# A fused attention and two-layer expert kernel: the issue order read from a table

## The chip, the cores and the metric

The kernel runs on one core of a Trainium2 chip. It is one program for five engines: TensorE (matmuls), VectorE (DVE in the rows), ScalarE (ACT), GpSimd (POOL) and SyncE (SP, which issues most DMAs); GpSimd issues a few DMAs too. Each engine takes its instructions in the order in which they are written, and waits where one needs what another engine has not finished. The metric is the device time of one execution in microseconds.

## The reference

```python
# attention, q, k, v: (4 batches, 8 heads, 576, 64)
q_d = q.reshape(B, H, 144, 4, D).mean(axis=3)          # k_d, v_d alike
out_up = np.repeat(sm_attn(q_d, k_d, v_d), 4, axis=2)   # softmax attention on 144 positions
mask = np.abs(pos[:, None] - pos[None, :]) < 4          # local attention
out_local = softmax(where(mask, q @ k.T / 8, -1e9)) @ v
x = (out_up + out_local)                                # -> (2304, 512)
h = (x @ w1) * (x @ w2) @ w3                            # w1, w2: 512x1024, w3: 1024x1024
y = h @ w_out                                           # w_out: 1024x512
z = maximum(maximum(y @ m1, y @ m2), y @ m3)            # 512x768 each
result = z @ m_out                                      # 768x512
```

The weights come as 64-bit numbers; the kernel turns them into 32-bit ones itself.

## The kernel before

All numbers are 32 bits wide. A matmul of full accuracy is written as three, of a high and a low part of each operand (`mm3`, L421 to L424), so most work goes in threes, 504 columns of x at a time (4 chunks of 504 and one of 288).

The program is built twice over. First Python code walks through the work and adds some 2,500 *tasks* to a list (`Program.add`), each with an engine, a cost, a function that issues its instructions, and the tasks it depends on. Then `Program.order` decides in which order the tasks are issued, and the functions are called in that order. So the place of an instruction in the code says nothing about when it runs. `order` in this kernel is a list scheduler: it steps through planned time, and each engine takes the ready task with the earliest due time; the due times come from a backward pass and a table of shifts, one for each group of tasks (`SHIFTS`).

The stages of work:

- *Tiles of the down-sampled attention* (`down`, one for each batch and pair of heads, sixteen in all). One `qk` load (576 KB); a `vd` tile that is loaded once by SP and then added to three times by accumulating DMAs of GpSimd (L476); the copies `q` and `k` (ScalarE, L484), the sums `qk` (VectorE, L489 and L491), scores `sp` on TensorE (L501), maxima (L511), `two`, which holds four maxima and sums for each row (L514, L525, L527), the exponentials (L518), scaling `e` (L531), transposes `pp` (L540), output `po` (L550).
- *Slabs of the local attention* (`slab`, three a batch, 192 columns each): value loads (`v` and `vl`), scores `sq` (L604), softmax on VectorE and ScalarE, transposes `ptq` (L630), outputs `poq` (L649), sum with the tile's output (L658), and the split into high and low part, `xt` (L415 on ScalarE, L417 on VectorE).
- *W' = w3 @ w_out* (`weights_product`), which replaces two matmuls of the reference by one: twelve weight blocks of 128x1024 (`raw`, loaded 512 KB at a time) are converted (`float32`, L442 on ScalarE, L443 to L448 on VectorE) into `wf`, and sixteen products `pw` (L711) of four logical matmuls (eight instructions) each are summed in two halves; each half is then split into `wp`.
- *First layer*: for each chunk and each of eight blocks f, `pf` (two matmul groups, `front`), their product `g`, and `py` (`back`), with weights `w` that `pair` converts. The first `pf` needs x of columns 0 to 503, that is the first three slabs, and the first pair of weights.
- *Second layer*: weights `cv` are converted, summed and written to memory (`convert`), fetched again (`wu`), and used in products `pb` (`halves_front`, `rest_front`), and at the end `final` with `gg` and `wm`.

Tasks marked `chained` (the products of W', of the first layer and of the second) depend on the one added before: they run on TensorE in the order in which they are added, W' first. All matmuls of the attention are free to stand between them.

Buffers: four PSUM banks for sums and four for the rest in the first stages; two `qk` buffers, three `vd` buffers, six places for raw weight blocks, two places for a slab's values. A load into a buffer waits on its queue until the buffer's last reader is done, and whatever stands behind it on that queue waits too.

Of the kernel before, what the change touches and what calls it, by code (L numbers as in the profile page):

```python
# [17 lines left out]
HP = H // 2  # L18
# [49 lines left out]
ROUNDS_PLAIN = 6  # L68

SHIFTS = {  # L70
# [72 lines left out]
class Task:  # L143
    __slots__ = ("n", "options", "fn", "deps", "nexts", "late", "end", "size", "takes", "tiles", "group", "count")


class Program:


    AFTER = {"PE": 0.30, "DVE": 0.12, "ACT": 0.15, "POOL": 0.15, "SP": 2.2}  # L150
    RATE = 0.32e6
    ADDS = 2.3

    HAND, COME = 165, 70

    def __init__(self):
        self.tasks, self.chain, self.group = [], None, 0

    def add(self, options, fn, reads=(), writes=(), chained=False, size=0, count=0):
# [3 lines left out]
        t.n, t.options, t.fn, t.size, t.group = len(self.tasks), options, fn, size, self.group  # L163
        t.count = count
        t.nexts, t.end, t.late, t.takes, t.tiles = [], None, None, [], []
        deps = set()
# [28 lines left out]
    def order(self, rounds=ROUNDS_PLAIN):  # L195

        ts = self.tasks
        for t in ts:
            for d in t.deps:
                ts[d].nexts.append(t.n)  # L200
        for t in reversed(ts):
            t.late = min((ts[n].late - self.lag(t, t.options, n) for n in t.nexts), default=0.0)
            t.late -= min(c for _, c in t.options) + t.size / self.RATE
        best = None
        for n in range(rounds):
            done, places = self.forward()
            end = max(t.end for _, _, t, _ in done)
            if best is None or end < best[0]:
                best = end, done, places, [t.late for t in ts]
            self.backward(done)  # L210
        for t, late in zip(ts, best[3]):
            t.late = late + SHIFTS.get(t.group, 0.0)
        best = None, *self.forward()
        for x, slot in best[2]:
            x.slot = slot
        return [(t, e) for _, _, t, e in sorted(best[1], key=lambda d: d[:2])]

    def lag(self, task, options, n):

        (e, _), *more = options  # L220
        if task.size:
            return self.AFTER["SP"] + (self.ADDS if e == "POOL" else 0.0)
        to = self.tasks[n].options
        return 0.0 if not more and len(to) == 1 and e == to[0][0] != "SP" else self.AFTER[e]

    def backward(self, done):
        ts = self.tasks
        on = {t.n: e for _, _, t, e in done}
        left = [len(t.nexts) for t in ts]
        by = [0.0] * len(ts)  # L230
        free, queue = dict.fromkeys(self.AFTER, 0.0), 0.0
        can = {e: [n for n in on if on[n] == e and not left[n]] for e in self.AFTER}
        for _ in ts:
            now, e, n = None, None, None
            for o, ns in can.items():
                if ns:
                    at = min(free[o], max(by[n] for n in ns))
                    if now is None or at > now:
                        now, e = at, o
            n = max((n for n in can[e] if by[n] >= now), key=lambda n: (ts[n].end, n))  # L240
            t = ts[n]
            can[e].remove(n)
            cost = dict(t.options)[e]
            if t.size:
                queue = min(queue, now) - t.size / self.RATE
                t.late = queue - cost
                free[e] = min(free[e], now) - cost
            else:
                t.late = free[e] = now - cost
            for d in t.deps:  # L250
                left[d] -= 1
                by[d] = min(by[d], t.late - self.lag(ts[d], [(on[d], 0)], n))
                if not left[d]:
                    can[on[d]].append(d)

    def forward(self):
        ts = self.tasks
        for t in ts:
# [4 lines left out]
        left = [len(t.deps) for t in ts]  # L263
        can = {e: set() for e in self.AFTER}
        free = dict.fromkeys(can, 0.0)
        ready = [0.0] * len(ts)
        queue = 0.0
        hand, since = self.HAND, 0.0
        places, done = [], []

        def offer(t):
            for e, _ in t.options:
                can[e].add(t.n)

        def start(n):
            t = ts[n]
            if t.count:
                return max(free["PE"], begin(n), since + (t.count - hand) / self.COME - t.options[0][1])
            return begin(n)

        def begin(n):
            t = ts[n]
            if not t.takes:
                return ready[n]
            return max(ready[n], sorted(s.free for s in t.takes[0].among)[len(t.takes) - 1])

        for t in ts:
            if not t.deps:
                offer(t)
        while len(done) < len(ts):  # L290
            best = None
            for e, ns in can.items():
                if not ns:
                    continue
                at = {n: start(n) for n in ns}
                now = max(free[e], min(at.values()))
                if now < 1e9 and (best is None or now < best[0]):
                    best = now, e, min((n for n in ns if at[n] <= now), key=lambda n: (ts[n].late, n))
            now, e, n = best
            t = ts[n]  # L300
            if len(t.options) > 1:

# [9 lines left out]
            for o, _ in t.options:  # L312
                can[o].discard(n)
# [15 lines left out]
            for m in t.nexts:  # L329
                left[m] -= 1  # L330
                ready[m] = max(ready[m], end + self.lag(t, [(e, 0)], m))
                if not left[m]:
                    offer(ts[m])
# [867 lines left out]
```

## Time and profile before

| what | value |
|---|---|
| runs | 780.63, 780.65, 784.3 us; median 780.65 |
| profiled execution, span | 781.2 us |
| TensorE (PE) busy | 734.0 us, 94% |
| VectorE busy | 482.0 us, 62% |
| ScalarE busy | 324.1 us, 41% |
| GpSimd busy | 53.7 us, 7% |
| chain that ended last | PE 83%, DVE 6%, DMA 5%, ACT 2%, issue 1%, SPq 1% |
| DMA | 126.99 MB, mean 163 GB/s |

The profiled execution's own time is its span, from the first instruction to the last. Busy time is the share in which an engine worked; a wait in the timeline stands in brackets behind the instruction that ended it, with what it waited for. One logical matmul of W' shows as two instructions. An average over the span hides that the engines are loaded differently early and late, so the rows below are by stretch.

### The profile page before, as it was taken

How to read it: one execution, taken by the hardware profiler on the slowest of the kernel's cores; microseconds unless marked ns; L12 is line 12 of the kernel's file. 1: busy time of each engine (PE TensorE's matmuls, PEld its weight loads, DVE VectorE, ACT ScalarE, POOL GpSimd, SP SyncE). 2: the span in 40 equal slices, each digit the busy share in tenths (PEclk: the TensorE clock that was granted, in tenths of full speed). 3: DMA queues.
4: the chain of work that ended last, by engine and by line, in shares of the span. 5: the costliest groups of instructions: out<-in, count | busy, mean ns of one | idle time of the engine just before them, and what ended most of it. 6: DMA issues, size and time to landing. Idle time of an engine off the chain costs nothing.

```text
span 781.2 us, 15778 instructions
## 1 busy us (share of the span) xinstructions
PE 734.0 (94%) x6404; PEld 575.3 (74%) x6404; DVE 482.0 (62%) x843; ACT 324.1 (41%) x704; POOL 53.7 (7%) x130
## 2 busy tenths in 40 slices
PE   0596899999999999999999999999999999999997
PEld 0243446777778777877888899888887888878886
DVE  3889688786354523241576769878867742676322
ACT  3655546755673663241343455532233101125321
POOL 2203110330022010000000000000000000000000
PEclk9995899999999999999999999999999999999999
DMA  8995545322352111111557567585777863377213
GB/s 208 344 359 152 143 140 176 93 58 42 88 154 47 52 47 28 54 27 25 164 189 262 195 232 260 174 303 206 270 266 254 307 223 108 129 227 226 87 61 121
DMA packets 63192, 126.99 MB, mean 163 GB/s; under 512 B 23376, under 2 KB 43856, under 8 KB 60432
## 3 DMA queue, kind: packets, MB, share of 16 engines
q1 hardware_dynamic: 58512, 122.45, 46.2%
q0 software_dynamic: 4608, 3.55, 3.3%
q8 instruction: 50, 0.82, 0.4%
q14 instruction: 22, 0.18, 0.1%
HBM read 87.43 MB, written 38.54 MB: 161 GB/s over the span
## 4 chain that ended last, share of the span: by engine, by line
PE 83%; DVE 6%; DMA 5%; ACT 2%; issue 1%; SPq 1%; POOL 0%; ACTq 0%; DVEq 0%
PE pb L422 11%; PE pb L424 10%; PE pb L423 10%; PE pf L422 9%; PE pf L423 8%; PE pf L424 8%; PE py L422 5%; PE pw L711 5%; PE py L423 4%; PE py L424 4%; PE poq L649 2%; PE sq L604 2%; DVE t L876 1%; DMA w_dram<-hls 1%; PE sp L501 1%
## 5 line engine op out<-in xcount | busy, mean ns | idle before, releaser
L422 PE MATMUL pb<-xc,wu 128*128 128x504 f32 (+1 forms) x324 | 120.5, 372 | 2.1 <-DVE t L876 1.9
L422 PE MATMUL pf<-xt,w 128*128 128x504 f32 (+1 forms) x320 | 120.7, 377 | 0.1
L424 PE MATMUL pb<-xc,wu 128*128 128x504 f32 (+1 forms) x324 | 119.8, 370 | 0.0
L423 PE MATMUL pb<-xc,wu 128*128 128x504 f32 (+1 forms) x324 | 119.6, 369 | 0.0
L423 PE MATMUL pf<-xt,w 128*128 128x504 f32 (+1 forms) x320 | 118.8, 371 | 0.0
L424 PE MATMUL pf<-xt,w 128*128 128x504 f32 (+1 forms) x320 | 118.8, 371 | 0.0
L744 DVE TENSOR_TENSOR z<-pf,z 128x504 f32<-128x504 f32 (+1 forms) x40 | 25.5, 636 | 80.3 <-PE pf L424 60.8
L422 PEld LDWEIGHTS pb<-xc,wu 128*128 128x128 f32 x324 | 60.9, 188 | 15.8 <-DVE t L876 5.9
L422 PEld LDWEIGHTS pf<-xt,w 128*128 128x128 f32 x320 | 60.1, 188 | 11.7 <-issue 1.0
L423 PEld LDWEIGHTS pb<-xc,wu 128*128 128x128 f32 x324 | 61.0, 188 | 10.0
L424 PEld LDWEIGHTS pb<-xc,wu 128*128 128x128 f32 x324 | 60.8, 188 | 10.1
L711 PE MATMUL pw<-wf 128*128 128x512 f32 x128 | 64.9, 661 | 3.6 <-DVE wf L448 3.6
L424 PEld LDWEIGHTS pf<-xt,w 128*128 128x128 f32 x320 | 60.2, 188 | 10.4
L423 PEld LDWEIGHTS pf<-xt,w 128*128 128x128 f32 x320 | 60.2, 188 | 9.5
L422 PE MATMUL py<-g,wp 128*128 128x504 f32 (+1 forms) x160 | 64.2, 401 | 0.0
L876 DVE TENSOR_TENSOR t<-t,pb 128x504 f32<-128x504 f32 x60 | 40.5, 677 | 36.6 <-PE pb L424 32.0
L423 PE MATMUL py<-g,wp 128*128 128x504 f32 (+1 forms) x160 | 59.4, 372 | 0.4 <-DVE g L417 0.4
L878 ACT COPY t<-pb 128x504 f32<-128x504 f32 x36 | 20.9, 580 | 93.1 <-PE pb L424 92.6
L424 PE MATMUL py<-g,wp 128*128 128x504 f32 (+1 forms) x160 | 59.2, 370 | 0.0
L711 PEld LDWEIGHTS pw<-wf 128*128 128x128 f32 x128 | 26.0, 211 | 34.4 <-issue 30.0
L742 ACT COPY z<-pf 128x504 f32<-128x504 f32 (+1 forms) x40 | 21.7, 543 | 58.1 <-PE pf L424 58.0
L422 PE MATMUL pb<-gg,wm 128*128 128x504 f32 (+1 forms) x120 | 44.6, 372 | 0.2 <-DMA wm<-m_dram 0.2
(117 smaller groups left out, 1208.0 us busy)
## 6 DMA issues: line engine op xcount, KB each, us to landing
wu<-w_dram SPq DMA_DIRECT2D x18, 1024.0 KB
w_dram<-hl SPq DMA_DIRECT2D x20, 512.0 KB
qk<-qkp SPq DMA_DIRECT2D x16, 576.0 KB
raw<-m SPq DMA_DIRECT2D x18, 512.0 KB
raw<-w3t SPq DMA_DIRECT2D x16, 512.0 KB
raw<-w SPq DMA_DIRECT2D x16, 512.0 KB
w_dram<-hls SPq DMA_DIRECT2D x16, 512.0 KB
area<-g_dram SPq DMA_DIRECT2D x24, 252.0 KB
```

Of the source, the lines that this page charges most:

```text
L422: nc.tensor.matmul(o, wlo, xhi, start=first, stop=False, skip_group_check=again)
L423: nc.tensor.matmul(o, whi, xlo, start=False, stop=False, skip_group_check=again)
L424: nc.tensor.matmul(o, whi, xhi, start=False, stop=last, skip_group_check=again)
L501: e.matmul(sps[a]()[:KH, half * GD:(half + 1) * GD], s()[h, half * KH:(half + 1) * KH], s()[h, GD:2 * GD], start=True, stop=True,)
L604: e.matmul(sps[a]()[j * 32:(j + 1) * 32, (half * HP + hp) * BK:(half * HP + hp + 1) * BK], q[h, t:t + 32], k[h, t:t + BK], start=True, sto ...
L649: e.matmul(pos[hp]()[a * D:(a + 1) * D, i * BQ:(i + 1) * BQ], vw()[h, a, i], pt().rearrange("p a n -> p (a n)")[h, c:c + BQ], start=True, ...
L711: e.matmul(os[i](), w()[:, i * P:(i + 1) * P], o(), start=n == 0, stop=n == NF - 1)
L742: prog.add(act(n), lambda e, pp=pp: e.copy(z()[:, :n], pp()[:, :n]), [pp], [z])
L744: prog.add(psum(n), lambda e, pp=pp: e.tensor_tensor(z()[:, :n], pp()[:, :n], z()[:, :n], op=ALU.mult), [pp], [z])
L876: prog.add(dve(N), lambda e: e.tensor_tensor(ap(o), ap(x), ap(y), op=op), [x, y], [o])
L878: copy = lambda o, x: prog.add(act(N), lambda e: e.copy(ap(o), ap(x)), [x], [o])
```

## The change

The scheduler goes. `ORDER` holds, for each engine, the numbers of all tasks in the order in which they are to be issued (584 on TensorE, 858 on VectorE, 558 on ScalarE, 96 on GpSimd, 443 on SP). `order` now only walks through the five lists in planned time, to interleave them in one program and to choose buffers where a task may use one of several. Its costs are new (`act`, `dve`, `AFTER`, `RATE` and others), and it counts a lower TensorE clock after a pause; since the order of each engine is given, these numbers move nothing in an engine's order (they can pick another of several buffers). `chained` becomes a named chain: the products of W' form the chain "W", everything else the chain "x", and each `py` depends on the last product of W'. The `two` multiply (L525) goes from GpSimd to VectorE.

```diff
-SHIFTS = {
-    1: -3810.3, 2: -904.2, 3: -133.1, 4: -40, 5: 20.9, 6: -3404.5, 7: -4191.5, 8: -83.8, 9: -38, 10: -56.5, 11:
...
+ORDER = {
+    "PE":
+    "12 307 21 23 308 39 116 309 25 310 117 48 50 66 311 312 52 77 75 93 313 79 127 314 151 104 102 152 106 129 "
...
-    AFTER = {"PE": 0.30, "DVE": 0.12, "ACT": 0.15, "POOL": 0.15, "SP": 2.2}
-    RATE = 0.32e6
-    ADDS = 2.3
+    AFTER = {"PE": 0.16, "DVE": 0.12, "ACT": 0.15, "POOL": 0.15, "SP": 1.9}
+    RATE = 0.36e6
+    ADDS, MORE = 2.2, 4.5
...
+    BEGIN, PAUSE, HEAT = 0.8, 4.2, 4.5
...
-        if chained:
-            if self.chain is not None:
-                deps.add(self.chain)
-            self.chain = t.n
+        if chain is not None:
+            if chain in self.chains:
+                deps.add(self.chains[chain].n)
+            self.chains[chain] = t
...
+        queues = {e: [ts[int(n)] for n in reversed(ORDER[e].split())] for e in self.AFTER}
...
+        while len(done) < len(ts):
+            now, e = min(((start(e), e) for e in queues), key=lambda s: s[0])
+            t = queues[e].pop()
...
-    act = lambda n: [("ACT", 0.14 + n * 0.00098)]
-    dve = lambda n: [("DVE", 0.16 + n * 0.00104)]
+    act = lambda n: ("ACT", 0.03 + n * 0.00098)
+    dve = lambda n: ("DVE", 0.08 + n * 0.00104)
...
-        prog.add([("POOL", 0.25)], lambda e: e.tensor_scalar(
+        prog.add(("DVE", 0.1), lambda e: e.tensor_scalar(
             two()[:, 1], two()[:, 1], 4.0, 4e-9, op0=ALU.mult, op1=ALU.add), [], [two])
...
-                prog.add(pe(3.45), product, [dw, do], os, chained=True)
+                prog.add(pe(3.45), product, [dw, do], os, chain="W")
...
-            prog.add(mm(n, 3), products, [dw, g], [os[l]], chained=True)
+            prog.add(mm(n, 3), products, [dw, g], [os[l]], chain="x", after=[prog.chains["W"]])
```

What it moves, at three places. First TensorE's first steps, before: `sp` are scores of a tile, `pp` transposes of a tile, `sq` scores of the first slab, `pw` products of W', `po` a tile's output; "x20" is five products of four logical matmuls.

```order
L501 MATMUL sp<-qk 72x144 x4
L540 MATMUL pp<-ident,e 72x72 x8
L604 MATMUL sq<-area 32x32 x32
L501 MATMUL sp<-qk 72x144 x4
L711 MATMUL pw<-wf 128x512 x20
L604 MATMUL sq<-area 32x32 x16
L604 MATMUL sq<-k,q 32x32 x16
L711 MATMUL pw<-wf 128x512 x4
L550 MATMUL po<-dp,area 64x144 x4
```

And now (L530 is the old L501, L740 the old L711, L569 the old L540, L633 the old L604, L579 the old L550):

```order
L530 MATMUL sp<-qk 72x144 x4
L740 MATMUL pw<-wf 128x512 x4
L569 MATMUL pp<-ident,e 72x72 x8
L740 MATMUL pw<-wf 128x512 x4
L530 MATMUL sp<-qk 72x144 x4
L633 MATMUL sq<-area 32x32 x32
L740 MATMUL pw<-wf 128x512 x4
L579 MATMUL po<-dp,area 64x144 x4
L740 MATMUL pw<-wf 128x512 x4
```

The first product stands right behind the first scores, and the products stand singly between the attention's steps; the first `po` has come from behind the sixth product to behind the third. The first `pf` still comes behind the sixteenth product in both lists.

Second the loads on SP, before: `qk` a tile's queries and keys, `raw` weight blocks of W' from `w3t` and `wo`, `vp` the first part of a `vd` tile (`area`, `vd`), `vl` and `v0` a slab's values.

```order
L390 DMA raw_136<-wo 128x1024 x2
L476 DMA area_134<-vp 72x256
L390 DMA qk_151<-qkp 128x1152
L390 DMA area_156<-vl 15x8x64 x8
L390 DMA area_156<-v0 15x2x512 x4
L390 DMA raw_176<-w3t 128x1024 x2
L390 DMA qk_180<-qkp 128x1152
L476 DMA area_143<-vp 72x256
L476 DMA vd_184<-vp 72x256
```

And now (L419 is the old L390, L505 the old L476):

```order
L419 DMA qk_134<-qkp 128x1152
L419 DMA raw_136<-w3t 128x1024
L505 DMA area_138<-vp 72x256
L419 DMA raw_140<-wo 128x1024
L505 DMA area_142<-vp 72x256
L419 DMA raw_140<-wo 128x1024
L419 DMA qk_145<-qkp 128x1152
L505 DMA vd_147<-vp 72x256
L419 DMA raw_149<-wo 128x1024
L419 DMA raw_136<-w3t 128x1024
L419 DMA raw_149<-wo 128x1024
L419 DMA raw_154<-w3t 128x1024 x2
```

The first tile's load comes first, the weights of the first products and three `vp` loads follow, and the twelve value loads of the second slab have gone behind them.

Third VectorE, from the first maxima to the first reciprocal, before: `qk` the sums of a tile, `two` maxima and sums, `wf` weights in conversion.

```order
L489 TENSOR_TENSOR qk_151<-qk_151 128x576
L491 TENSOR_TENSOR qk_151<-qk_151 128x288
L511 TENSOR_REDUCE two_218<-sp_209 72x2
L511 TENSOR_REDUCE two_218<-sp_211 72x2
L527 RECIPROCAL two_218<-two_218 72x4
L443 TENSOR_SCALAR wf_235<-wf_235 128x1024
L444 TENSOR_SCALAR wf_235<-wf_235 128x1024
L446 SCALAR_TENSOR_TENSOR wf_235<-raw_176,wf_235 128x1024
L448 SCALAR_TENSOR_TENSOR wf_235<-raw_176,wf_235 128x1024
```

And now (L518 is the old L489, L520 the old L491, L472 to L477 the old L443 to L448, L540 the old L511, L554 the old L525, L556 the old L527):

```order
L540 TENSOR_REDUCE two_197<-sp_175 72x2
L540 TENSOR_REDUCE two_197<-sp_177 72x2
L518 TENSOR_TENSOR qk_145<-qk_145 128x576
L520 TENSOR_TENSOR qk_145<-qk_145 128x288
L472 TENSOR_SCALAR wf_157<-wf_157 128x512
L473 TENSOR_SCALAR wf_157<-wf_157 128x512
L475 SCALAR_TENSOR_TENSOR wf_157<-raw_136,wf_157 128x512
L477 SCALAR_TENSOR_TENSOR wf_157<-raw_136,wf_157 128x512
L554 TENSOR_SCALAR two_197<-two_197 72x4
L556 RECIPROCAL two_197<-two_197 72x4
```

The four-value multiply (L554) stands on VectorE right ahead of the reciprocal, and the sums of the second tile have moved ahead of it.

## Rows read from the trace of the kernel before

**Rows 1.** Windows of the whole execution (start:end, length; busy per engine, instructions; clock; DMA)

```profile
core 0: us, PE busy (x) PEld busy (x) DVE busy (x) ACT busy (x) POOL busy (x), PEclk, DMA share, GB/s
0.00:13.40 13.40, 0.00 (x0) 0.00 (x0) 5.66 (x11) 5.05 (x6) 5.40 (x32) 1.00 0.75 173
13.40:61.40 48.00, 32.51 (x232) 15.93 (x232) 37.50 (x54) 27.18 (x49) 6.62 (x9) 1.00 0.96 326
61.40:78.50 17.10, 11.55 (x101) 6.36 (x99) 15.62 (x24) 9.31 (x33) 7.23 (x9) 0.50 0.58 163
78.50:88.70 10.20, 9.27 (x270) 5.59 (x268) 8.29 (x17) 5.52 (x13) 1.94 (x3) 1.00 0.52 137
88.70:95.50 6.80, 3.98 (x23) 1.85 (x23) 4.55 (x8) 6.01 (x7) 1.24 (x8) 0.50 0.48 97
95.50:127.70 32.20, 32.20 (x400) 15.78 (x399) 26.54 (x48) 14.63 (x32) 2.61 (x8) 1.00 0.42 140
127.70:776.40 648.70, 644.50 (x5388) 529.79 (x5386) 383.33 (x683) 256.01 (x564) 28.61 (x62) 1.00 0.46 152
776.40:781.30 4.90, 0.00 (x0) 0.00 (x0) 0.56 (x2) 0.42 (x2) 0.00 (x0) 1.00 0.49 176
```

**Rows 2.** Timeline of TensorE, head (start, duration, instruction, idle before)

```profile
13.46 1.24 PE L501 MATMUL sp<-qk 64*72 64x144 f32 x8 [13.46 <-DVE qk L491]
...
32.24 20.04 PE L711 MATMUL pw<-wf 128*128 128x512 f32 x40 [3.62 <-DVE wf L448]
...
66.93 1.73 PE L540 MATMUL pp<-ident,e 72*72 72x72 f32 x8 [5.41 <-ACT e L531]
...
73.23 6.29 PE L711 MATMUL pw<-wf 128*128 128x512 f32 x8
...
80.67 3.65 PE L711 MATMUL pw<-wf 128*128 128x512 f32 x8
...
127.75 0.48 PE L422 MATMUL pf<-xt,w 128*128 128x504 f32 x1
```

**Rows 3.** Timeline of VectorE, head

```profile
22.12 0.17 DVE L527 RECIPROCAL two<-two 72x4 f32<-72x4 f32 x1 [6.58 <-POOL two L525]
...
51.99 0.69 DVE L443 TENSOR_SCALAR wf<-wf 128x1024 f32<-128x1024 f32 x1
...
55.85 0.69 DVE L443 TENSOR_SCALAR wf<-wf 128x1024 f32<-128x1024 f32 x1
...
124.86 1.16 DVE L417 TENSOR_TENSOR xt<-x,xt 128x240 fp32r<-128x240 f32 x4
```

**Rows 4.** Timeline of ScalarE, first 18 us

```profile
4.54 0.66 ACT L442 ACTIVATE wf<-raw 128x512 f32<-128x512 f32 x1 [2.31 <-DMA raw<-wo]
6.10 0.67 ACT L442 ACTIVATE wf<-raw 128x512 f32<-128x512 f32 x1 [0.90 <-DMA raw<-wo]
9.88 2.24 ACT L484 COPY area<-qk 128x576 f32<-128x576 f32 x2 [3.12 <-DMA qk<-qkp]
...
17.17 0.20 ACT L518 ACTIVATION_READ_ACCUMULATOR e<-sp,two 72x1 f32 x1
```

**Rows 5.** Timeline of SP, the queue that issues most loads

```profile
0.74 0.85 SPq L390 DMA_DIRECT2D raw<-wo  x2
...
2.51 7.69 SPq L390 DMA_DIRECT2D area<-vl  x8
```

**Rows 6.** Timeline of GpSimd, head

```profile
21.00 0.83 POOL L476 DMA_DIRECT2D area<-vp  x1 [7.83 <-DMA area<-vp]
21.90 0.18 POOL L525 TENSOR_SCALAR two<-two 72x4 f32<-72x4 f32 x1
...
61.77 1.45 POOL L476 DMA_DIRECT2D area<-vp  x1 [18.23 <-PE po L550]
```

**Rows 7.** Loads by line, with their sizes

```profile
qk<-qkp SPq DMA_DIRECT2D x16, 576.0 KB
...
raw<-wo SPq DMA_DIRECT2D x8, 512.0 KB
```

More of the change, by code (lines that the diff above doesn't have):

```diff
@@ L143, with add @@
 class Task:
-    __slots__ = ("n", "options", "fn", "deps", "nexts", "late", "end", "size", "takes", "tiles", "group", "count")
+    __slots__ = ("n", "e", "cost", "fn", "deps", "nexts", "end", "size", "takes", "tiles", "group", "count", "dense")
 class Program:
-    AFTER = {"PE": 0.30, "DVE": 0.12, "ACT": 0.15, "POOL": 0.15, "SP": 2.2}
-    RATE = 0.32e6
-    ADDS = 2.3
+    AFTER = {"PE": 0.16, "DVE": 0.12, "ACT": 0.15, "POOL": 0.15, "SP": 1.9}
+    RATE = 0.36e6
+    ADDS, MORE = 2.2, 4.5
     HAND, COME = 165, 70
+    BEGIN, PAUSE, HEAT = 0.8, 4.2, 4.5
     def __init__(self):
-        self.tasks, self.chain, self.group = [], None, 0
-    def add(self, options, fn, reads=(), writes=(), chained=False, size=0, count=0):
+        self.tasks, self.chains, self.group = [], {}, 0
+    def add(self, on, fn, reads=(), writes=(), chain=None, size=0, count=0, after=()):
         t = Task()
[L163 to L166, printed above, removed]
+        t.n, (t.e, t.cost), t.fn, t.size, t.group = len(self.tasks), on, fn, size, self.group
+        t.count, t.dense = count, chain is not None
+        t.nexts, t.end, t.takes, t.tiles = [], None, [], []
+        deps = {d.n for d in after}
         for what, writing in ((reads, False), (writes, True)):
@@ L193, in add, with order @@
         return t
-    def order(self, rounds=ROUNDS_PLAIN):
+    def order(self):
         ts = self.tasks
+        queues = {e: [ts[int(n)] for n in reversed(ORDER[e].split())] for e in self.AFTER}
+        free = dict.fromkeys(queues, self.BEGIN)
+        left = [len(set(t.deps)) for t in ts]
+        ready = [0.0] * len(ts)
         for t in ts:
@@ L200, in order @@
                 ts[d].nexts.append(t.n)
[L201 to L254, printed above, removed]
@@ L281, in begin @@
[L281 to L289, printed above, removed]
-        while len(done) < len(ts):
[L291 to L301, printed above, removed]
-                def end(o, c):
-                    return max(free[o], ready[n]) + c + sum(
-                        ts[m].options[0][1] for m in can[o]
-                        if m != n and len(ts[m].options) == 1 and ready[m] <= now and o == "DVE")
-                _, _, e, cost = min((end(o, c), i, o, c) for i, (o, c) in enumerate(t.options))
-                now = max(free[e], ready[n])
-            else:
-                cost = t.options[0][1]
-            for o, _ in t.options:
-                can[o].discard(n)
@@ new lines, in order, with start @@
+        last, heat, cold = -99.0, 0.0, True
+        done = []
+        def start(e):
+            if not queues[e] or left[queues[e][-1].n]:
+                return 1e9
+            t = queues[e][-1]
+            at = max(free[e], ready[t.n])
+            if t.takes:
+                at = max(at, sorted(s.free for s in t.takes[0].among)[len(t.takes) - 1])
+            if t.count:
+                at = max(at, since + (t.count - hand) / self.COME - t.cost)
+            return at
+        while len(done) < len(ts):
+            now, e = min(((start(e), e) for e in queues), key=lambda s: s[0])
+            t = queues[e].pop()
+            cost = t.cost
+            if e == "PE":
+                if now - last > self.PAUSE:
+                    cold, heat = True, 0.0
+                if cold and not t.dense:
+                    cost = cost * 1.5
+                elif cold:
+                    need = self.HEAT - heat
+                    if 2 * cost <= need:
+                        cost = 2 * cost
+                        heat = heat + cost
+                    else:
+                        cost = need + (cost - need / 2)
+                        cold = False
+                if t.dense:
+                    last = now + cost
@@ L320, in forward @@
                 hand, since = min(self.HAND, hand + self.COME * (end - since)) - t.count, end
-            if t.size:
-                queue = end = max(queue, now) + t.size / self.RATE
-            t.end = end + (self.lag(t, [(e, 0)], None) if t.size else self.AFTER[e])
+            if not t.size:
+                t.end = end + self.AFTER[e]
+            elif e == "POOL":
+                t.end = end + self.ADDS + min(max(0.0, queue - now), self.MORE)
+                queue = max(queue, now) + t.size / self.RATE
+            else:
+                queue = max(queue, end) + t.size / self.RATE
+                t.end = queue + self.AFTER["SP"]
             for x in t.tiles:
@@ L327, in forward @@
                     x.slot.free = max(ts[m].end for m in x.tasks)
-            done.append((now, len(done), t, e))
+            done.append(t)
             for m in t.nexts:
                 left[m] -= 1
-                ready[m] = max(ready[m], end + self.lag(t, [(e, 0)], m))
-                if not left[m]:
-                    offer(ts[m])
-        return done, places
+                same = not t.size and ts[m].e == e != "SP"
+                ready[m] = max(ready[m], end if same else t.end)
+        return done
 @with_exitstack
@@ L507, in down @@
         ex = er.tile([KH, 4, GD], F32, "e")
-        prog.add(pe(0.55), scores, [s], [*sps, ex])
+        prog.add(pe(0.77), scores, [s], [*sps, ex])
         two = twor.tile([KH, 2, 4], F32, "two")
@@ L513, in down @@
                 [sps[a]], [(two, a)])
-        prog.add(act(3), lambda e: e.mul(two()[:, 0], two()[:, 0], -SCALE / 16.0), [], [two])
+        prog.add(("ACT", 0.24), lambda e: e.mul(two()[:, 0], two()[:, 0], -SCALE / 16.0), [], [two])
         def exponentials(e, a):
@@ L531, in normalise @@
                 e.mul(ex()[:, w], ex()[:, w], two()[:, 1, w:w + 1])
-        prog.add([("ACT", 1.12)], normalise, [two], [ex])
+        prog.add(("ACT", 1.24), normalise, [two], [ex])
         pt = dpr.tile([KH, 2, 2, GD], F32, "dp")
@@ L607, in scores @@
                             )
-            prog.add(pe(0.65), scores, [x for hp in range(part * HP // 2, (part + 1) * HP // 2) for x in planes[b, hp]],
+            prog.add(pe(0.78), scores, [x for hp in range(part * HP // 2, (part + 1) * HP // 2) for x in planes[b, hp]],
                      [*sps, st] if part == 0 else sps, count=128)
@@ L653, in values @@
                             )
-            prog.add(pe(0.65), values, [vw, pt, ods[b]], [*pos, *x32s] if half == 0 else pos, count=128)
+            prog.add(pe(0.92), values, [vw, pt, ods[b]], [*pos, *x32s] if half == 0 else pos, count=128)
         for h2, x32 in enumerate(x32s):
@@ L738, in products @@
                     mm3(pp()[:, :n], w()[:, 0, c], w()[:, 1, c], x[:, 0, k % 2, :n], x[:, 1, k % 2, :n], k == 0, k == KX - 1)
-            prog.add(mm(n, 12), products, [dw, *xt], [pp], chained=True)
+            prog.add(mm(n, 12), products, [dw, *xt], [pp], chain="x")
             if i == 0:
@@ L864, in products @@
                 mm3(pp()[:, :N], w()[:, i % 4, 0, c], w()[:, i % 4, 1, c], at(0, k), at(1, k), first and k == 0, k == 1, not first)
-        prog.add(mm(N, 6), products, [w, *tiles], [pp], chained=True)
+        prog.add(mm(N, 6), products, [w, *tiles], [pp], chain="x")
     def halves_front(unit, w, x, zs, temps, G, p):
@@ L927, in products @@
                         k == 0, k == KX - 1)
-            prog.add(mm(n, 12), products, [a, *rest], [pp], chained=True)
+            prog.add(mm(n, 12), products, [a, *rest], [pp], chain="x")
             if w == 0:
@@ L962, in products @@
                         mm3(pp()[:, :n], wp(0), wp(1), g[f2]()[:, f % 2, 0, :n], g[f2]()[:, f % 2, 1, :n], f == 0, f == NF2 - 1)
-                prog.add(mm(n, 6), products, [ms[f2], g[f2]], [pp], chained=True)
+                prog.add(mm(n, 6), products, [ms[f2], g[f2]], [pp], chain="x")
             first = ch * N // BQ
@@ L1095, in attention_moe_kernel @@
     with tc.manual_schedule():
-        for t, e in order:
-            t.fn(engines[e])
+        for t in order:
+            t.fn(engines[t.e])
 def kernel(**inputs):
```

62 lines of the change are left out of this document (23 added, 39 removed), and 131 rows, old and new, of tables (ORDER, SHIFTS).

## The prediction

> **What bounds the kernel now.** I read the windows of busy time first [rows 1], then the timelines of TensorE, VectorE, ScalarE and the two issuing queues over the first 128 us [rows 2 to 6]. The windows cut the execution in two. From 127.7 to 776.4 us TensorE is busy 644.5 of 648.7 us at the granted clock 1.00: only 4.2 us are open there, and after 776.4 us there is a tail of 4.9 us. Before 127.7 us TensorE is busy 89.5 us (0 + 32.51 + 11.55 + 9.27 + 3.98 + 32.20), so 38.2 us are open, and some of the busy time is spent at the lower clock, 0.50 (1.2 GHz), in two stretches of 17.1 and 6.8 us [rows 1]. What the change can win is in this head.
>
> The head ends when the first `pf` matmul starts, at 127.75 us [rows 2]. It needs x of columns 0 to 503, which is the last VectorE work before it (the `xt` differences, 124.86 to 126.0 us, [rows 3]). VectorE is busy 98.2 us up to there (5.66 + 37.50 + 15.62 + 8.29 + 4.55 + 26.54, [rows 1]), more than TensorE. So VectorE is the fullest engine of the head, with 29.5 us idle; TensorE waits for chains that pass through it.
>
> Three of the waits can be read. First, TensorE does nothing until 13.46 us, when the `qk` sums come [rows 2]: the `qk` load landed only at 9.88 [rows 4], behind two weight loads and beside eight `vl` loads whose issue took SP from 2.51 to 10.2 us [rows 5]. Second, the four-value multiply `two` on GpSimd: ScalarE had finished the exponentials at 17.37 us [rows 4], but `two` ran at 21.90, since a `vp` load stood before it in GpSimd's queue and went out only at 21.00 [rows 6]; VectorE's reciprocal at 22.12 shows 6.58 us idle for it [rows 3]. Third, the first W' product starts at 32.24 [rows 2]. At 66.93 the engine had been idle 5.41 us, and the product that starts at 73.23 takes 6.29 us for its eight matmuls, against 3.65 at 80.67 [rows 2].
>
> **The change, part by part.** The instructions are the same but for one: sixteen `two` multiplies leave GpSimd for VectorE. Nearest row: the reciprocal on the same 72x4 tile, 0.17 us [rows 3]. I take that, between nothing (it falls into a moment in which VectorE waits) and 0.36 us (twice the 0.18 that GpSimd took, [rows 6]): the five in the head cost 0 to 1.8 us, I count 0.85. What it gives back is the wait behind the `vp` load: 21.90 - 17.37 = 4.5 us on the first tile.
>
> W' in its own chain: with the table given, all sixteen products still stand before the first `pf`, as before. The freedom itself is not used; it costs and gives nothing.
>
> So the order is the change. I count it at the first `pf`, engine by engine.
>
> *Arrival.* Two 512 KB loads issued from 0.74 us let ScalarE start at 4.54 and at 6.10 [rows 4, 5, 7]: 1.56 us per 512 KB, and 2.24 us before the first. Now `qk` (576 KB) is first: it lands at 0.74 + 2.24 + 1.76 = 4.7. ScalarE copies it with one weight instruction between the copies (two copies take 2.24, [rows 4]) and ends at about 8.2; VectorE starts its first conversion at 7.0 and ends the sums at 10.5. First TensorE work at 10.6 instead of 13.46.
>
> *First product.* It needs two half conversions. Six loads stand up to its last one: 576 + 3 x 512 + 2 x 72 KB = 2,256 KB (a `vp` load is 72x256 numbers of 4 bytes), which land at 0.74 + 2.24 + 4.41 x 1.56 = 9.9. VectorE's list to that point is 7.2 us long: product 1 starts at about 14.4 instead of 32.24.
>
> *VectorE up to the first `pf`.* One conversion of a 128x1024 block takes 55.85 - 51.99 = 3.86 us [rows 3]. Before, sixteen of them stand ahead (twelve for W', four for the first weights), 61.8 of the 98.2 us; 36.4 us are the rest. Now fifteen stand ahead: 57.9. Of the rest 3.7 us move behind (the sums of a later tile 1.2, three weight differences 2.05, one x difference 0.45), and 2.2 come forward (two weight differences, five `two`). So 57.9 + 34.9 = 92.8 us. Starting at 7.0, VectorE could be done at 99.8 if it never waited.
>
> *TensorE up to the first `pf`.* Of the 89.5 us busy, 11.55 + 3.98 lie at 0.50 and would be half as long at the full clock, 7.8 less; the block of five products from 32.24 took 20.04 where five at 3.65 are 18.25, 1.8 less [rows 1, 2]. That leaves 79.9 us of work, and from 10.6 it gives 90.5 if TensorE never waited.
>
> *What is late next.* VectorE's list says when each pair of products can start, since product n needs its blocks. Counted in its list, four, eight and twelve blocks of 3.86 us stand ahead of products 3, 7 and 11, with 4.8, 11.6 and 22.6 us of the rest: 20.2, 42.5 and 68.9 us. From 7.0, with half a microsecond of stalls, these are 28, 50 and 76.4 us. TensorE reaches product 3 at about 27, product 7 at 48.6, and product 11 at 74; so it waits some 1 to 4 us at each, and once about 3.6 us before the second slab's transposes. After product 11 it has dense work to 103 (six products, two slabs' small matmuls), and VectorE's last x differences end at 102 to 104. Both give a first `pf` at 104.6 us. For the clock I add 2.5: the product at 73.23 lost 6.29 - 3.65 = 2.64 us that way after a wait of 5.41. That is 107. VectorE is then idle about 7 us after its start at 7.0, instead of 24.
>
> *Queues moved past.* SP's list now holds the `qk` load of the fourth tile in front of the next weights, and it must wait for the second tile's scores (27 us); behind it the weights of products 7 and 8 land at about 32 to 37 and are wanted at 42. SP later holds the value loads of the third slab, which wait for the first slab's output products (about 62 us); behind them come the second and third weight blocks for `pf`, wanted at 84. Both are covered by 5 to 15 us; if that cover goes, the shift is one to one.
>
> *Behind the first `pf`.* The chain of `pf` and `py` is fixed in both orders; 4.2 us are open now. VectorE has less in reserve, because TensorE arrives 20 us earlier while the next weights still need 3.86 + 1.3 us each. I allow 0 to 10 us and take 2, near the present 4.2 in total. The tail is unchanged.
>
> *Sum.* 127.75 - 107 = 20.7 gained in the head, 2 given back, and 0.65 for one scores step that now stands ahead of the first `pf` (1.24 us in the cold row at 13.46, [rows 2], about half of it at the full clock): 781.2 - 20.7 - 0.65 + 2 = 761.8 of span. The span of the profiled execution stands 0.55 us above the median of the runs, 780.65; so about 761 us.
>
> **Rivals.**
>
> *A. Given back later.* In the 41 us after the first `pf` VectorE's list is about 35 us long, against 38 for the 50 us before. With three partners and a fixed order a fill of 85% may not hold. For it: from 61.4 to 78.5, at a fill of 91% (15.62 of 17.1, [rows 1]), TensorE stood idle 5.41 us. Against: from 127.7 on hardly anything waited. It gives back the whole 10 us: 770.
>
> *B. The value loads decide.* The product `po` of the first tile now stands between products 3 and 4; before it came behind product 6. It needs three accumulating `vp` loads by GpSimd, each after the landing of the last; the third went out at 21.00 [rows 6], so the tile is complete at 27 to 30, and now two other tiles' loads stand between. TensorE gets there at 31.7. If each step takes 3 us more, TensorE, SP (whose next load waits for `po`) and then VectorE slip by up to 9 us: 770. A `vp` issue took 0.83 us at 21.00 and 1.45 at 61.77, while VectorE ran [rows 6]. The Trainium skill (SBUF — State Buffer, Who interferes with whom) says that VectorE in its two-port modes locks GpSimd out of the shared port, so that such loads wait for their descriptors; the longer row agrees, and a fuller VectorE would meet it more often.
>
> *C. The lower clock, slower than before.* Before, five products ran as one block from 32.24, 20.04 us, and a product caught at the lower clock cost 6.29 [rows 2]. Now products stand singly or in twos, between small matmuls and waits. If the clock stays at 0.50, a product costs between that 6.29, whose end came after the rise at 78.5, and twice 3.65; with 6.85 it is 3.2 more. Sixteen are 51 us, of which the waits for VectorE and the 2.5 already charged cover some 12: 761 + 39 = 800. It decides once 21 / 3.2, six to seven, products lie at the lower clock where no wait covers them. Against it: each product is itself 3.6 us of dense work, and the block from 32.24 lost only 1.8 us, though TensorE had done little before it. The Trainium skill (TensorE: Matmul & The Clock Gate, A second HAM failure mode) tells of a kernel whose short idle times between groups made the clock swing; the drop at 88.7 us, with a wait of 2.8 us behind it, is the nearest thing here.
>
> *D. It does nothing.* The old order was set by a planner too; the new one may only exchange waits. 781. Against it: the 13.46, 6.58 and 5.41 us are waits whose causes the new order takes out.
>
> **How the numbers follow.** Forecast 0.62 (757 to 767), A or B 0.20, C 0.07, D 0.05; 0.06 for better than the forecast (VectorE with no idle at all, 99.8: 753). About 0.5%, 3.9 us, is what a measurement of this kernel can tell from no change. Faster by more than that: forecast, A, B and better, 0.88; within it D, 0.05; slower C, 0.07. The range from 752 to 775 leaves out C, D and a little of A and B.
>
> **What would show it.** Right: first scores near 10.6 us and the first product near 14.4; the first `pf` at 104 to 111; VectorE busy over 85% from 7 us to there; the stretch from the first `pf` to the last matmul within 3 us of 648.7. Wrong: a first `pf` after 115 us, a granted clock of 0.50 over more than 20 us after the first product, or more than 10 us open on TensorE behind the first `pf`.

## The result and the profile after

The changed kernel takes 754.73 us (median of four runs, 753.59 to 757.28); beside it the kernel before took 781.79. The ratio is 0.9661, 95% interval 0.963 to 0.9692. The forecast was 761, with a range of 752 to 775. The profiled execution has a span of 755.5 us, 25.7 less than before.

The windows, cut at the first scores, at the two edges of the longer stretch at the lower clock, at the first `pf` and at the last matmul (columns as in [rows 1]):

```profile
0.00:10.60 10.60, 0.00 (x0) 0.00 (x0) 3.23 (x8) 5.71 (x7) 4.15 (x21) 1.00 0.83 279
10.60:61.60 51.00, 45.29 (x428) 22.61 (x428) 48.70 (x79) 35.57 (x87) 12.51 (x25) 0.97 0.92 286
61.60:71.90 10.30, 8.01 (x131) 4.62 (x132) 8.77 (x17) 2.13 (x3) 0.00 (x0) 0.50 0.95 301
71.90:104.50 32.60, 32.60 (x474) 16.67 (x473) 30.47 (x54) 20.23 (x39) 4.86 (x11) 1.00 0.55 142
104.50:751.40 646.90, 642.34 (x5378) 528.85 (x5376) 381.21 (x704) 252.12 (x571) 26.75 (x58) 1.00 0.48 156
751.40:755.60 4.20, 0.00 (x0) 0.00 (x0) 0.41 (x3) 0.00 (x0) 0.00 (x0) 0.88 0.41 151
```

The head, up to the first `pf`, went from 127.75 to 104.54 us: 23.2 of the 25.7 us. In it TensorE is busy 85.9 us (45.29 + 8.01 + 32.60, before 89.5 in [rows 1]) and VectorE 91.2 us (3.23 + 48.70 + 8.77 + 30.47, before 98.2). VectorE's idle time after its first conversion fell from some 24 to some 6 us. Behind the first `pf` TensorE still never waits for long: 4.56 us are open, before 4.2; its work there is 2.2 us shorter and the tail 0.7.

TensorE's timeline in the head, against [rows 2]:

```profile
10.67 1.24 PE L530 MATMUL sp<-qk 64*72 64x144 f32 x8 [10.67 <-DVE qk L520]
14.45 5.09 PE L740 MATMUL pw<-wf 128*128 128x512 f32 x8 [2.54 <-DVE wf L477]
...
20.67 3.65 PE L740 MATMUL pw<-wf 128*128 128x512 f32 x8
...
27.18 5.40 PE L740 MATMUL pw<-wf 128*128 128x512 f32 x8 [1.54 <-DVE wf L477]
32.51 0.72 PE L579 MATMUL po<-dp,area 72*64 72x144 f32 x8
...
49.64 3.70 PE L740 MATMUL pw<-wf 128*128 128x512 f32 x8 [0.48 <-DVE wf L477]
...
65.08 1.32 PE L678 MATMUL poq<-pt,area 30*64 30x24 f32 x75 [2.27 <-issue]
66.33 6.44 PE L740 MATMUL pw<-wf 128*128 128x512 f32 x8
...
73.83 7.13 PE L740 MATMUL pw<-wf 128*128 128x512 f32 x16
...
104.54 0.50 PE L451 MATMUL pf<-xt,w 128*128 128x504 f32 x1
```

The first product runs at 14.45 us instead of 32.24, and the waits are short ("issue" is a wait for nothing that the profile shows). From 66.33 us on TensorE waits for nothing up to the first `pf`. VectorE, against [rows 3]:

```profile
7.37 0.43 DVE L472 TENSOR_SCALAR wf<-wf 128x512 f32<-128x512 f32 x1 [6.50 <-ACT wf L471]
...
18.66 0.17 DVE L556 RECIPROCAL two<-two 72x4 f32<-72x4 f32 x1
...
66.41 0.62 DVE L687 TENSOR_TENSOR x<-poq,od 128x192 f32<-128x192 f32 x2 [1.40 <-PE poq L678]
...
102.27 0.73 DVE L446 TENSOR_TENSOR xt<-x,xt 128x240 fp32r<-128x240 f32 x2 [0.20 <-ACT xt L444]
```

The 6.58 us in front of the reciprocal are gone, and the last `xt` differences end at 103.0, 1.5 us ahead of the first `pf`: both engines reach that point nearly together. ScalarE, SP and GpSimd, against [rows 4 to 6]:

```profile
4.57 1.17 ACT L513 COPY area<-qk 128x576 f32<-128x576 f32 x1 [2.33 <-DMA qk<-qkp]
```

```profile
0.74 0.39 SPq L419 DMA_DIRECT2D qk<-qkp  x1
```

```profile
7.23 1.10 POOL L505 DMA_DIRECT2D area<-vp  x1 [3.15 <-DMA area<-vp]
14.17 1.70 POOL L505 DMA_DIRECT2D area<-vp  x2 [5.65 <-DMA area<-vp]
```

The `qk` load lands at 4.57 us, 5.3 us earlier. (A row of two DMA instructions gives the time of both.)

### The profile page after: what moved, and what is told of

Its sections match the earlier page's. It is cut to its first block, busy times and chain, and to the rows that moved or that the text cites. A ratio compares the mean times of both kernels' runs of the same rounds, so it can differ in the third digit from the quotient of the medians.

```text
span 755.5 us, 15650 instructions
## 1 busy us (share of the span) xinstructions
PE 728.2 (96%) x6404; PEld 572.8 (76%) x6404; DVE 472.8 (63%) x859; ACT 315.8 (42%) x704; POOL 48.3 (6%) x114
## 4 chain that ended last, share of the span: by engine, by line
PE 86%; DVE 6%; DMA 5%; issue 2%; ACT 0%; SPq 0%; ACTq 0%; DVEq 0%
PE pb L451 11%; PE pb L452 11%; PE pb L453 10%; PE pf L451 9%; PE pf L453 9%; PE pf L452 9%; PE py L451 5%; PE pw L740 5%; PE py L452 4%; PE py L453 4%; PE poq L678 3%; PE sq L633 2%; DMA raw<-w3t 2%; DMA wu<-w_dram 1%; PE po L579 1%
## 5 line engine op out<-in xcount | busy, mean ns | idle before, releaser
L451 PEld LDWEIGHTS pf<-xt,w 128*128 128x128 f32 x320 | 60.1, 188 | 11.6 <-ACT dp L572 1.1
L740 PE MATMUL pw<-wf 128*128 128x512 f32 x128 | 64.2, 652 | 4.6 <-DVE wf L477 4.6
L453 PEld LDWEIGHTS pf<-xt,w 128*128 128x128 f32 x320 | 60.1, 188 | 10.3
L740 PEld LDWEIGHTS pw<-wf 128*128 128x128 f32 x128 | 25.4, 208 | 33.7 <-issue 27.1
L452 PE MATMUL pb<-gg,wm 128*128 128x504 f32 (+1 forms) x120 | 44.6, 372 | 0.0
L451 PE MATMUL pb<-gg,wm 128*128 128x504 f32 (+1 forms) x120 | 44.4, 370 | 0.0
```

The costliest lines, as they stand in the source:

```text
L451: nc.tensor.matmul(o, wlo, xhi, start=first, stop=False, skip_group_check=again)
L452: nc.tensor.matmul(o, whi, xlo, start=False, stop=False, skip_group_check=again)
L453: nc.tensor.matmul(o, whi, xhi, start=False, stop=last, skip_group_check=again)
L740: e.matmul(os[i](), w()[:, i * P:(i + 1) * P], o(), start=n == 0, stop=n == NF - 1)
```

## The experiments

Theory: the new order of the head makes the gain. It starts VectorE early and keeps it supplied, and VectorE and TensorE then bound the head almost equally. Rivals: the multiply on VectorE; the new order behind; TensorE alone. Four kernels contain the changed head nearly as it is (the change, e2, e3, e7); their first `pf` lies at 104.5, 103.0, 103.1 and 104.8 us, so a single trace tells about 2 us. The kernel before, measured beside each group of runs, has medians from 780.63 to 782.09 us, so a loss of 5 us against the change is clear and one of 1 us is not. In the edits the numbers are tasks.

**e1, the multiply alone.** The earlier order of every engine, written into the changed program's table, with `two` on VectorE right ahead of the reciprocal. So the named chains, the new costs and their choice of buffers are in it too; of the edit only the multiply is shown here.

```diff
-        prog.add([("POOL", 0.25)], lambda e: e.tensor_scalar(
+        prog.add(("DVE", 0.1), lambda e: e.tensor_scalar(
```

> The order of before on every engine, with one edit: the sixteen two multiplies stand on VectorE, each right ahead of its reciprocal. Theory (the order of the loads and of VectorE's list makes the gain): VectorE no longer stands idle 6.58 us at its first reciprocal, but its next weights land only at about 19.7 us, so 2 to 4 us come back there and some of it is lost again; 776 to 781 us, ratio 0.993 to 1.000. Rival (the wait of the multiply behind the vp load is the main thing): at least 10 us, 771 or less, ratio under 0.987.

Measured 780.19 us, ratio 0.9994 (0.9971 to 1.0017). VectorE's timeline:

```profile
17.55 0.17 DVE L557 RECIPROCAL two<-two 72x4 f32<-72x4 f32 x1
19.74 0.69 DVE L473 TENSOR_SCALAR wf<-wf 128x1024 f32<-128x1024 f32 x1 [2.01 <-ACT wf L472]
```

The reciprocal comes 4.6 us earlier than in [rows 3], and VectorE then waits for weights. The first `pf` is at 126.2; the time is the same. Neither the multiply nor the program around the table is the gain.

**e2, the multiply back on GpSimd,** in the new order.

```diff
-        prog.add(("DVE", 0.1), lambda e: e.tensor_scalar(
+        prog.add(("POOL", 0.25), lambda e: e.tensor_scalar(
```

> The new order with one edit: the sixteen two multiplies go back to GpSimd, each at the place in its list that the plan's time gives it, between the vp loads. Theory (order): 0 to 3 us more than the changed kernel, 754 to 758 us, ratio 0.965 to 0.970. Rival (the multiply on VectorE is the main thing): 765 us or more, ratio over 0.979.

755.03 us, ratio 0.9685 (0.9654 to 0.9717): nothing is lost. With e1 the multiply is worth nothing either way.

**e3, the new head with the earlier order behind.** Every list is the new one to the first `pf` (601), then the remaining tasks as they stood before.

```diff
 "PE": "... 450 448 466 601"
-"603 607 609 613 614 615 452 ..."
+"452 603 607 609 613 614 615 ..."
```

> The new lists on every engine up to the issue of the first pf, and from there the remaining tasks in the order of before (two on VectorE). Theory (all of the gain lies ahead of the first pf): first pf at 104 to 106 us, 754 to 759 us, ratio 0.964 to 0.972. Rival (the new order wins behind the first pf too, or the old tail is made for the old head and stalls): 765 us or more.

766.24 us, ratio 0.9821 (0.9791 to 0.9851): a miss; the second half of the rival, an old tail that stalls, held. The head is as new, but TensorE (first row) stops behind it, for ScalarE (other rows):

```profile
114.01 0.79 PE L452 MATMUL pf<-xt,w 128*128 128x504 f32 x1 [7.28 <-ACT z L771]
```

```profile
108.78 1.14 ACT L445 CAST w<-cv 128x512 fp32r<-128x512 f32 x2 [4.08 <-DVE cv L478]
109.83 2.25 ACT L514 COPY area<-qk 128x576 f32<-128x576 f32 x2
...
113.37 0.59 ACT L771 COPY z<-pf 128x504 f32<-128x504 f32 x1
```

In the earlier order a weight cast, waiting for VectorE, and two tile copies stand ahead of the `z` copy that frees the bank of `pf`. In the medians 11.5 us of the gain are given back. In the traces the span behind the first `pf` is 659.3 us against 651.0 in the change, 8.3 us longer; this one wait is 7.28 of them.

**e4, the earlier head with the new order behind** (the reverse join).

```diff
 "PE": "12 21 23 116 39 ... 601"
-"452 603 466 607 609 613 614 615 ..."
+"603 607 609 613 614 615 452 616 ..."
```

> The lists of before up to the issue of the first pf (two on VectorE), and from there the remaining tasks in the new order. Theory (all of the gain lies ahead of the first pf): as the order of before with two on VectorE, 776 to 782 us, ratio 0.993 to 1.001. Rival (the order behind the first pf has a part in the gain): 771 us or less.

779.27 us, ratio 0.9995 (0.997 to 1.0019), first `pf` at 129.84, and 652.9 us behind it (before 653.45). Behind the earlier head the new order gives nothing.

**e5 and e6, VectorE or TensorE relieved.** e5 cuts the OR of the low words to four columns in the twelve W' blocks; e6 issues half of twelve products.

```diff
-            u(), low(), 29, u(), op0=ALU.logical_shift_right, op1=ALU.bitwise_or), [words], cv)
+            few(u()), few(low()), 29, few(u()), op0=ALU.logical_shift_right, op1=ALU.bitwise_or), [words], cv)
...
-                    for i in range(4):
+                    for i in range(4 if n in (0, NF - 1) else 2):
```

> The new order with the wide OR that inserts the low words cut from full width to 4 columns for the twelve W' conversion blocks that use it (so the low words of W' are left out of the result); about 12.9 us of VectorE work go from the head. Theory (VectorE, dense from 7.4 us to 102.6 us, bounds the head about as much as TensorE, whose floor there is about 90): the first front matmul moves from 104.5 us to 93-98 us, and the run takes 744 to 750 us. Rival (TensorE and its clock alone bound the head): first front matmul within 1.5 us of 104.5, run 753 to 757 us.

> The new order with twelve of the sixteen W' products issuing two of their four matmuls (half of these products' sums is left out of the result); about 21 us of TensorE work go from the head. Theory (VectorE bounds the head too): the first front matmul still starts at 102 to 104.5 us and the run takes 752 to 756 us. Rival (TensorE alone bounds the head): first front matmul at 84 to 92 us, run 735 to 743 us.

One run each: e5 751.29 us, above its forecast of 744 to 750, e6 754.08. With one run the place of the first `pf` tells more than the time. The first `pf` of e5, then of e6:

```profile
99.42 0.49 PE L452 MATMUL pf<-xt,w 128*128 128x504 f32 x1
```

```profile
103.40 0.50 PE L452 MATMUL pf<-xt,w 128*128 128x504 f32 x1 [0.37 <-ACT dp L573]
```

In e5 VectorE works 79.6 us up to there instead of 91.2, but the first `pf` moves by 5 us only, a little less than the theory had: TensorE, dense from 61.87 us on, becomes the bound. In e6 TensorE works 74.5 us up to there instead of 85.9, 11.4 us less where 21 were left out; the mean granted clock up to the first `pf` is 0.87 instead of 0.93, which took part of it. The first `pf` moves by nothing that can be told, and VectorE is as full as before (90.9 us). TensorE alone is not the bound.

**e7, the seam at 190 us.** As e3, but new up to a front matmul of the second chunk (893).

```diff
 "PE": "... 741 764 883 887 888 889 890 891 766 782"
-"893 897 768 898 899 840 ..."
+"768 840 791 793 841 795 ..."
```

> The new lists as far as a front matmul of the second chunk (about 190 us), the earlier order of issue from there on. Theory (the whole gain is made up to there; the 11 us lost with the seam at the first front matmul came from the order directly behind it): 753 to 758 us, ratio 0.964 to 0.971. Rival (the earlier order behind does not fit this head wherever the seam lies): 762 us or more, with a wait of 4 us or more on TensorE behind the seam.

767.64 us, ratio 0.983 (0.9812 to 0.9848): the rival held in the time, though not in its sign, one wait of 4 us or more; the longest is 2.81. So the loss isn't bound to the place directly behind the head. One window of e7, the same window of the change, and TensorE's longest wait in e7:

```profile
210.00:230.00 20.00, 14.01 (x320) 10.04 (x317) 7.57 (x19) 9.98 (x37) 5.03 (x6) 0.62 0.45 110
```

```profile
210.00:230.00 20.00, 20.00 (x225) 15.32 (x222) 7.32 (x18) 7.75 (x29) 5.10 (x6) 1.00 0.35 84
```

```profile
221.92 1.09 PE L660 MATMUL ptq<-ident,s 128*128 128x128 f32 x4 [2.81 <-DVE s L654]
```

In the change TensorE is busy for all of it at the clock 1.00. In e7 small products whose inputs are not ready come close together; 6.0 us are idle, and the granted clock falls to 0.62 on average. TensorE's busy time over the whole is 734.2 against 728.2 us. A join costs 11 to 13 us at either place.

**e8, the value loads ahead again.** Twelve loads of the second slab (139 to 150) in SP's list behind the first `qk`, one `raw` and one `vp`.

```diff
-"220 1 214 28 213 27 55 ..."
+"220 1 139 140 142 143 145 146 148 149 141 144 147 150 214 28 213 27 55 ..."
```

> The new order with the twelve value loads of the second slab put ahead on SP's queue again, behind the first qk load and one raw and one vp load, as they stood before. Theory (the early weights start VectorE and the W' products early): weights land about 9 us later, the second W' product and VectorE's conversions move by 5 to 9 us, first front matmul 109 to 113 us, run 760 to 764 us. Rival (the place of the value loads costs nothing, the loads share the bandwidth anyhow): within 1.5 us of the new order, 753 to 757 us.

763.05 us, ratio 0.9767 (0.9728 to 0.9806). TensorE's wait for the first product:

```profile
18.75 5.87 PE L741 MATMUL pw<-wf 128*128 128x512 f32 x8 [7.06 <-DVE wf L478]
```

The first product comes 4.3 us later and the first `pf` at 110.44, 5.9 later, and the run takes 8.3 us longer: the theory's numbers.

**e12, the first products in one block.** Products 307 to 311 in one block behind the second tile's `sp` (39) and the first slab's first `sq` step (116), as before. (The expectation calls both of these `sq`; the second `sq` step, 117, stands behind the block.)

```diff
-"12 307 21 23 308 39 116 309 25 310 117 48 50 66 311 312 ..."
+"12 21 23 39 116 307 308 309 310 311 25 117 48 50 66 312 ..."
```

> The new order, but with the first five W' products in one block behind both sq products, as they stood before, instead of one by one between the attention's products. Theory (placing them one by one keeps VectorE supplied, since it waits for attention products that stand behind the block): VectorE idles some 5 us more in the head, first front matmul 108 to 112 us, run 758 to 762 us. Rival (where the products stand is worth nothing, the early weights and the one first tile make the gain): first front matmul within 1.5 us of 104.5, run 753 to 757 us.

766.09 us, ratio 0.9795 (0.975 to 0.9839), first `pf` at 113.91: both above the theory's ranges, with about twice the loss expected. VectorE's wait, and the same step in the change:

```profile
45.75 0.76 DVE L642 TENSOR_TENSOR s<-sq,masks 128x256 f32<-128x256 f32 x2 [9.14 <-PE sq L634]
```

```profile
37.66 0.76 DVE L641 TENSOR_TENSOR s<-sq,masks 128x256 f32<-128x256 f32 x2 [1.00 <-PE sq L633]
```

VectorE stands 9.1 us for scores that lie behind the block. This is the largest loss that taking back one piece of the head brought. Only TensorE's list was taken back; VectorE's still expects the scores early, so part of the 9.1 us is the misfit of the two lists, and the runs don't tell how much.

**e9, e10 and e11, both bounds moved.** e9 takes the ninth product (323) and the splits that free its bank forward; e10 takes six VectorE operations of a later weight pair (364 to 367, 369, 371) behind the last `xt`, with the ScalarE instructions that belong to them; e11 does both.

```diff
 "PE":
-"152 106 129 130 323 162 ..."
+"152 106 323 129 130 162 ..."
 "DVE":
-"190 134 364 365 366 367 167 437 ..."
+"190 134 167 437 ..."
```

> The new order with the ninth W' product put ahead of the poq products that stand before it on TensorE, and the splits of the first W' half that free its bank put earlier on VectorE and ScalarE; TensorE is dense from that product to the first front matmul, so its bound moves earlier by some 4 us. Theory (VectorE, dense to 103 us, bounds the head within 2 us of TensorE): first front matmul 102.5 to 104.5 us, run 753 to 757 us. Rival (TensorE alone bounds): first front matmul 99 to 101 us, run 749 to 752 us.

> The new order with six VectorE operations (5.2 us) of a weight pair that is needed only behind the first front matmul put behind the last xt differences. Theory (both engines bound): first front matmul 103 to 104.5 us, set by TensorE from its ninth W' product at 66 us; run 752 to 757 us. Rival (VectorE alone bounds): first front matmul 98 to 100.5 us, run 748 to 752 us.

> Both moves together: ninth W' product and its splits earlier, and the six VectorE operations behind the xt differences. Theory (the two engines bound the head within 2 us of each other, so that only both moves together shorten it): first front matmul 97 to 101 us, run 747 to 752 us, ratio to the earlier kernel 0.957 to 0.963. Rival (the operations put back stall the front behind, or another engine ends the head): first front matmul as expected or later, run 753 us or more.

e9: 753.77 us, ratio 0.9637 (0.9612 to 0.9662), first `pf` 101.99, between the two expectations; no difference in time to the change that can be told. e10: 760.43, 0.973 (0.9704 to 0.9757), first `pf` 103.01. e11: 759.81, 0.9718 (0.9695 to 0.974), first `pf` 101.19. The theory wanted 102.5 to 104.5, 103 to 104.5 and 97 to 101. All three lie within 3.4 us of the change and within 2 us of e2 and e3, so that only both moves together shorten the head is not shown. e10 and e11 lose 5 to 6 us against the change, so the rival of e11 holds for the time. In e11 TensorE (first fence) waits for ScalarE:

```profile
109.34 0.50 PE L452 MATMUL pf<-xt,w 128*128 128x504 f32 x1 [2.40 <-ACT z L771]
```

```profile
106.66 2.16 ACT L472 ACTIVATE cv<-raw 128x1024 f32<-128x1024 f32 x2 [0.46 <-DVE w L447]
108.70 0.59 ACT L771 COPY z<-pf 128x504 f32<-128x504 f32 x1
```

The postponed conversions hold the next ones, and those stand in front of the `z` copy: what leaves the head returns behind it. The wait shown is 2.40 of the 5 us; directly behind it, from 110.60 to 114.00 us, the granted clock is 0.50. No version that does the whole work is shown to beat the change.

## Why the prediction was right, and where its size was off

*The head.* First scores were forecast at 10.6 us and came at 10.67; the first product at 14.4, came at 14.45; products 3, 7 and 11 at 28, 50 and 76.4, came at 27.18, 49.64 and about 77.4 (half of the pair from 73.83). VectorE's work was 91.2 us for 92.8 forecast, its last differences ended at 103.0 for 102 to 104. The walk's first `pf`, 104.6, was met at 104.54. That it was met so closely is luck in part: the four kernels with this head spread over 1.8 us, and on TensorE's side two errors cancel. From its first work on the walk gave TensorE 79.9 us of work and some 14 of waits; measured are 85.9 and 7.9. VectorE's side needs no such luck.

*The clock term failed.* The 2.5 us added on top had no place. Three products did run long, at 14.45, 27.18 and 66.33, 6.0 us over 3.65 together. At 27.18 and 66.33 the granted clock fell to 0.50; at 14.45 the rows show 1.00 throughout, so what slowed that product is open:

```profile
14.45:19.50 5.05, 5.05 (x9) 2.02 (x9) 4.88 (x12) 3.94 (x13) 2.71 (x10) 1.00 1.04 397
27.50:30.50 3.00, 3.00 (x5) 1.05 (x4) 2.93 (x5) 2.76 (x11) 2.31 (x2) 0.50 1.05 369
```

But of the waits that the walk gave TensorE at products 3, 7 and 11 and the second slab's transposes, only 1.54 and 0.48 us occurred, so the loss took the place of waits that the walk had counted already. The term counted it a second time.

*The 2 us given back failed too.* Span behind the first `pf`: 651.0 us for 653.45 before, 2.5 less instead of 1.35 more (2 less the 0.65). With the clock term that is 2.5 + 3.8 = 6.3, the whole distance between 761.8 and 755.5. The open time (4.56) and the tail (4.2) stayed near before. Of the 2.2 us less work, 0.65 were forecast. The rest is no more than traces of one order differ by: with the same order behind the first `pf`, TensorE works 641.9 us there in e12 and 644.2 in e9.

*The multiply.* The 4.5 us that it gives back are real at the reciprocal and worth nothing at the end (e1, e2); in e1 the wait for the next weights takes 2.01 of them. *W' in its own chain* was read from the order as unused; e1 has it with the earlier order and gains nothing.

*The rivals.* A, given back later, didn't happen in the change; e3, e7 and e10 show that its mechanism is near and what it costs, 5.7 to 12.9 us, where the order behind doesn't fit. B fell: the first `po` ran at 32.51 without a wait. A `vp` issue by GpSimd took between 0.83 us (at 23.27, with a `tensor_scalar` running on VectorE from 23.18 to 23.87) and 1.55 us (at 28.53, while the issue before it still ran), and no `po` of the head waited for a load. The Trainium skill (SBUF — State Buffer, Who interferes with whom) says that VectorE's two-port modes can hold up such issues; these rows neither bear that out nor rule it out. C fell: the stretches at 0.50 were 10.3 and some 3 us long, and two of sixteen products lay in them, not six. D fell.

*What made the gain.* Of the 23.2 us at the first `pf`, taking back the single placing of the products costs 9.4 (e12) and taking back the early weights 5.9 (e8), each with the other lists as in the change. The two need not add up; the rest wasn't taken apart. The ninth product shows where the gain is made. It starts at 66.33 us (before 91.82), and in all nine traces with this order behind it the first `pf` follows 37.1 to 38.5 us later, whether the ninth product came at 61.87 (e5) or 76.64 (e12). Neither engine relieved alone moves the head by what it is relieved of (e5, e6, one run each).

## What to carry to other kernels

Count for each engine its work up to the point at which the dense stretch begins, and what each step waits for; that walk gave the first `pf` within what one trace can tell, though TensorE's work and waits were each off by 6 us, while a surcharge on top of it was wrong. When two engines reach that point within 2 us of each other, relieving one of them buys little (11.6 us less on VectorE gave 5, 11.4 less on TensorE none). An issue order is one piece: the join of two orders cost 11 to 13 us, and six operations moved behind a boundary came back as 5 to 6 us, so try such a piece as a whole.

## What the runs showed of the hardware

Inside the 128 small `poq` matmuls in front of the ninth product TensorE stood 1.94 to 3.68 us, in each of the nine traces with the new head in that order, with nothing but "issue" to wait for; the product behind took 5.3 to 6.6 us instead of 3.70, at the granted clock 0.50 (1.2 GHz) in the change's window above. Where that product stood ahead of them (e9, e11) it took 3.70, and the 128 ran through in 1.46 us; an "issue" wait of 0.94 and 0.34 us came further on, among the `sq` matmuls. The kernel before has one of 2.82 us among its `sq` matmuls, at 91.53 us, and the product behind took 5.53. What the engine waits for there is open.

The length of a wait did not tell what it costs the product behind it. The third product ran 5.40 us behind waits of 1.54 (the change) and 1.26 us (e8), and 3.70 behind waits of 1.53 to 1.60 in e2, e3, e9, e10 and e11. In those five the seventh product ran 5.4 us, behind waits of 0.5 us, which cost it nothing in the change and e8 (3.70).
